# Totals of the softmax denominators by three bf16 products of exact pieces instead of one fp32 product

## The chip, the cores and the metric

The kernel runs on one core of a Trainium2 chip. A core has five engines with instruction queues of their own: PE (TensorE, matrix products into PSUM), DVE (VectorE), ACT (ScalarE), POOL (GpSimd) and SP (SyncE, which here issues most DMAs). They wait for each other by semaphores. The metric is the device time of one execution in microseconds; the time of the kernel before is the median of three runs.

## The reference, cut to what matters

Eight batches of eight heads, 576 positions and 64 values a head; a block-causal attention with blocks of 64, whose output is the input of a gated MLP without a nonlinearity.

```python
def _attn_ref(q, k, v):
    scores = scale * np.matmul(q, k.transpose(0, 1, 3, 2))
    scores = np.where(mask, scores, -1000000000.0)
    scores = scores - np.max(scores, axis=-1, keepdims=True)
    attn = np.exp(scores)
    attn = attn / (np.sum(attn, axis=-1, keepdims=True) + 1e-09)
    return np.matmul(attn, v)

def _moe_ref(x, w1, w2, w3, w_out):
    a = x @ w1
    b = x @ w2
    h = a * b @ w3
    return h @ w_out
```

The sum over the last axis of `attn` is the denominator that this case is about.

## The kernel before, in words

All products that need more than the rounded fp32 type of TensorE (`fp32r`) are made from a high and a low piece: `xh`, `xl` for the MLP's input, `w1h`, `w1l` for a weight, `ph`, `pl` for the exponentials. The work runs over 32 pairs of heads (`pair(n)`, four to a batch), and in a pair over its two heads `j`. Pairs 0 to 3 are "early": beside their attention the weights are unpacked and `w3 @ w_out` is multiplied out. From pair 4 on the attention of pair n runs beside the MLP of the batch before.

The order of PE is written out by hand: `PLAN` is a string of steps for each head, and each step takes one piece of work from a generator. `S` makes a tile of scores and its exponentials, `U` and `V` a piece of exponentials times values, `M` a piece of the row maxima of the next pair, `F` a piece of the MLP (24 a pair; half a batch of the MLP, 288 columns, is 48 of them: 32 of the two products `ab` at L426, then 16 of the product `o` at L442). `R`, `N` and `T` end a head: `R` is `sums`, `N` is `take`, `T` is `total`, `norm` and `finish_x`. The plan of the second head ends with `F R T M F F`. The other engines' instructions stand in the order in which the program issues them, as the scheduler places them.

The denominators from pair 4 on: POOL adds up the exponentials of a head in `rsum` (L286). `R` (L333, DVE) sums `rsum`, turned in blocks of 32 by 32, into 18 columns of `part`, one half for each head. `T` multiplies `part`, 128x36 in fp32, by `groups4` (four by four identities of 32x32 beside the identity, in the tile `ident`), which adds up the four groups of partitions into `tot` in PSUM (L337, PE). DVE copies `tot` into `rr` (L339), takes the reciprocal (L355), spreads it by a transpose (L357) and multiplies it into `x32` (L358); `finish_x` splits the result into `xh` and `xl` (L367 on ACT, L368 on POOL).

Around these stand: the row maxima `m` of the next pair (L196, L198 on DVE) and their transpose `mt` (L200, PE); `take` (L351 on ACT, L352 on DVE); the MLP's gate `g` (L433, DVE) with its high and low piece `gh` (L434, ACT) and `gl` (L435, POOL); the low piece of the queries and keys (L235, POOL, 64x1152) and of the values (L248, POOL).

Of the kernel before, what the change touches and what calls it, by code (L numbers as in the profile page):

```python
# [10 lines left out]
BF16 = mybir.dt.bfloat16  # L11
# [4 lines left out]
ALU = mybir.AluOpType  # L16
# [3 lines left out]
P = 128  # L20
B, H, S, D = 8, 8, 576, 64
# [46 lines left out]
def block_causal_attention__then__gated_mlp_kernel(ctx, tc, qkv, consts, ident_in, w1, w2, w3t, wout, out_t):  # L68
    nc = tc.nc
# [4 lines left out]
    work = ctx.enter_context(tc.tile_pool(name="work", bufs=1))  # L74
# [8 lines left out]
    ident, groups4 = both[:, 0:P], both[:, P:]  # L83
# [33 lines left out]
    tl = {}  # L117
# [9 lines left out]
    def open_late():  # L127
        pool = ctx.enter_context(tc.tile_pool(name="late", bufs=1, reuse_waits="tile"))
        tl["late"] = pool
        tl["ph"] = pool.tile([P, PW], F32R, name="ph")  # L130
        tl["sum"] = pool.tile([P, S], F32, name="rsum")
        tl["pl"] = pool.tile([P, PW], F32R, name="pl")

        tl["vs"] = [pool.tile([P, 5, P], F32R, name=f"vs{j}") for j in range(2)]
        tl["gh"] = pool.tile([P, NF, HALF], F32R, name="gh")
        tl["gl"] = pool.tile([P, NF, HALF], F32R, name="gl")
# [197 lines left out]

    def total(n, part, rr):
        tot = ps_q.tile([P, 512], F32, tag="psq", name=f"tot{n}")
        nc.tensor.matmul(tot[:, 0 : S // 16], groups4, part, start=True, stop=True)  # L337
        for j in range(2):
            nc.vector.tensor_scalar_add(rr[own[j]], tot[own[j], j * S // 32 : (j + 1) * S // 32], 1e-9)  # L339

# [127 lines left out]
    def pair(n):  # L468
# [9 lines left out]
        for j in range(2):  # L478
# [5 lines left out]
            for step in (EARLY_PLAN[n] if early else PLAN)[j].split():  # L484
# [3 lines left out]
                with tc.high_priority(offset=0) if early else nullcontext():  # L488
                    if step == "S":
                        fill(tiles, 1)  # L490
                    elif step == "F":
                        if delay:
                            delay -= 1
                        else:
                            fill(mlp, 1)
                    elif step == "M":
                        fill(masks, 1)
                    elif step == "A":
                        fill(next_qk, 1)
                    elif step == "B":  # L500
                        fill(own_qk, 1)
                    elif step in "UV":
                        fill(pvs, 1)
                    elif step == "R":
                        sums(n, j, part)
                    elif step == "N" and early:
                        take_early(n, j, xps, x32, rr)
                    elif step == "N":
                        take(n, j, xps, x32)
                    elif step == "T":  # L510
                        if not early:
                            total(n, part, rr)
                        norm(n, x32, rr)
                        finish_x(n, x32)
                    elif step == "Q" and not last:
                        if n + 1 != NPAIR:
                            prep_v(n + 1, j)
                        if j == 1 and n + 2 < NN:
                            load(n + 2)
# [4 lines left out]
    fill(prod, 100)  # L524
    wstack.close()
    open_late()
    for j in range(2):
        prep_v(NPAIR, j)
# [60 lines left out]
```

## Time and profile before

| what | value |
|---|---|
| median of three runs | 980.52 us (980.49 to 980.68) |
| the profiled execution | 982.55 us |
| its span, first to last instruction | 980.6 us |
| mean granted TensorE clock | 0.993 |
| from the `tot` of pair 4 (171.7 us) to that of pair 31 (896.7 us) | 27 pairs, 26.9 us each |
| `tot` (L337), two passes a pair | 56 products, 234 ns median each, beside 56 weight loads of 188 ns |
| L333, the reduction into `part` | 56, 43.0 us in all |
| L339, `tot` into `rr` | 56, 175 ns median |

A row of the profile's timeline gives the start in us from the beginning of the span, the duration, the engine, the line of the kernel, the operation, the tiles written and read, the shapes, how many instructions were merged into the row, and in brackets how long the engine stood idle before it and what released it. Products on PE overlap: a product of 288 columns is shown with 0.29 us and the next starts 0.13 us behind it. PEld rows are the loads of the weights, beside PE.

### The profile page before, as it was taken

The numbers are of one execution on the slowest core, as the hardware profiler recorded it, in microseconds if no ns is written. First come the engines' busy times: TensorE is split into PE (matmuls) and PEld (weight loads), VectorE is DVE, ScalarE is ACT, GpSimd is POOL, SyncE is SP. The second block draws the span as 40 slices with busy tenths as digits, with TensorE's granted clock in tenths as the row PEclk, the third lists the DMA queues.
The fourth block names the chain that finished last, engine by engine and source line by source line (L and its number), as shares of the span: only waits on it lengthen the run. The fifth ranks groups of instructions, "written<-read, shape, count | busy, mean of one in ns | idle before, by whom it ended". The sixth has DMA issues, their size and how long they took to land.

```text
span 980.6 us, 18312 instructions
## 1 busy us (share of the span) xinstructions
PE 941.6 (96%) x6594; PEld 879.1 (90%) x6624; DVE 692.4 (71%) x1230; ACT 557.3 (57%) x1451; POOL 629.6 (64%) x605
## 2 busy tenths in 40 slices
PE   3788989999999999999999999999999999999998
PEld 1444449999999999999999999999999999999998
DVE  6776857777777778878777777788787877774100
ACT  6776635656556665566565556655656555553221
POOL 6786737767676767677676767676776767673211
PEclk9999989999999999999999999999999999999999
DMA  8967502222222221222222221211222222100000
GB/s 294 304 198 221 163 19 62 63 75 63 87 63 75 63 87 41 66 69 65 73 66 83 64 80 57 88 54 53 69 72 66 69 81 63 50 13 25 7 19 25
DMA packets 31303, 79.81 MB, mean 81 GB/s; under 512 B 5356, under 2 KB 13676, under 8 KB 31212
## 3 DMA queue, kind: packets, MB, share of 16 engines
q1 hardware_dynamic: 29788, 76.26, 25.4%
q10 hardware_dynamic: 1424, 2.38, 1.0%
q8 instruction: 52, 0.85, 0.4%
q14 instruction: 39, 0.32, 0.1%
HBM read 50.76 MB, written 9.44 MB: 61 GB/s over the span
## 4 chain that ended last, share of the span: by engine, by line
PE 88%; ACT 3%; DVE 3%; POOL 3%; issue 2%; DMA 1%; ACTq 0%; SPq 0%; POOLq 0%; DVEq 0%
PE ab L426 42%; PE o L442 21%; PE s L265 9%; PE x L320 9%; PE mx L192 3%; PE w L407 2%; POOL wbits L152 1%; ACT wbits L151 1%; DMA wraw<-in_w 1%; ACT wy L150 1%; POOL w2l L162 1%; PE x L304 1%; DVE m L196 1%; ACT pe L273 1%; DVE qk L166 0%
## 5 line engine op out<-in xcount | busy, mean ns | idle before, releaser
L286 POOL TENSOR_TENSOR rsum<-rsum,p 128x448 f32<-128x448 f32 x224 | 186.1, 831 | 87.1 <-ACT p L280 76.8
L435 POOL TENSOR_TENSOR gl<-g,gh 128x288 fp32r<-128x288 f32 x128 | 114.5, 895 | 121.5 <-ACT gh L434 121.5
L283 DVE TENSOR_TENSOR pl<-p,ph 128x448 fp32r<-128x448 f32 x168 | 149.1, 901 | 60.1 <-ACT ph L281 59.2
L265 PE MATMUL s<-qk 128*128 128x288 f32 (+4 forms) x768 | 157.3, 314 | 16.3 <-ACT pe L273 10.8
L235 POOL TENSOR_TENSOR qk<-raw,qk 64x1152 fp32r<-64x1152 f32 x58 | 154.9, 2670 | 9.1 <-issue 6.1
L426 PE MATMUL ab<-xh,w2h 128*128 128x288 f32 x512 | 153.8, 300 | 0.0
L442 PE MATMUL o<-gh,wh 128*128 128x288 f32 x512 | 153.6, 300 | 0.0
L426 PE MATMUL ab<-xh,w1h 128*128 128x288 f32 x512 | 151.1, 295 | 0.0
L426 PE MATMUL ab<-xl,w2h 128*128 128x288 f32 x512 | 151.0, 295 | 0.0
L426 PE MATMUL ab<-xl,w1h 128*128 128x288 f32 x512 | 151.0, 295 | 0.0
L426 PE MATMUL ab<-xh,w1l 128*128 128x288 f32 x512 | 151.0, 295 | 0.0
L442 PE MATMUL o<-gh,wl 128*128 128x288 f32 x512 | 150.9, 295 | 0.0
L426 PE MATMUL ab<-xh,w2l 128*128 128x288 f32 x512 | 150.9, 295 | 0.0
L442 PE MATMUL o<-gl,wh 128*128 128x288 f32 x512 | 150.8, 295 | 0.0
L265 PEld LDWEIGHTS s<-qk 128*128 128x128 f32 (+1 forms) x768 | 116.9, 183 | 28.5 <-ACT pe L273 16.1
L434 ACT CAST gh<-g 128x288 fp32r<-128x288 f32 x128 | 55.4, 433 | 142.8 <-DVE g L433 142.7
L281 ACT ACTIVATE ph<-s 128x288 fp32r<-128x288 f32 x336 | 131.4, 393 | 0.0
L196 DVE TENSOR_REDUCE m<-mx 128x1 f32<-128x64 f32 (+3 forms) x320 | 128.3, 446 | 3.0 <-PE mx L192 0.8
L280 ACT ACTIVATE p<-s 128x448 f32<-128x448 f32 x224 | 85.5, 382 | 51.5 <-PE s L265 50.7
L283 DVE TENSOR_TENSOR pl<-rsum,ph 128x288 fp32r<-128x288 f32 x112 | 75.7, 677 | 49.2 <-ACT ph L281 45.4
L320 PE MATMUL x<-ph,vs 128*128 128x128 f32 x336 | 110.4, 329 | 0.0
L433 DVE TENSOR_TENSOR g<-ab,a 128x288 f32<-128x288 f32 x128 | 56.5, 441 | 69.5 <-PE ab L426 68.6
(76 smaller groups left out, 2182.4 us busy)
## 6 DMA issues: line engine op xcount, KB each, us to landing
raw<-in_qkv SPq DMA_DIRECT2D x31, 896.0 KB
qk<-qk SPq DMA_DIRECT2D x108, 144.0 KB
out_t<-o SPq DMA_DIRECT2D x64, 144.0 KB
wraw<-in_w3t SPq DMA_DIRECT2D x16, 512.0 KB
wraw<-in_w SPq DMA_DIRECT2D x16, 512.0 KB
wraw<-in_wout SPq DMA_DIRECT2D x8, 512.0 KB
qk<-qk ACTq DMA_DIRECT2D x16, 144.0 KB
qk<-ms SPq DMA_DIRECT2D x54, 2.2 KB
```

Source lines behind the costliest of these rows:

```text
L196: nc.vector.reduce_max(m[:, col : col + 1], sc, axis=AX.X)
L235: (nc.gpsimd if "late" in tl or n * j else nc.vector).tensor_tensor(out=qk[j][o, 2:4], in0=rqk[o], in1=qk[j][o, 0:2], op=ALU.subtract)
L265: nc.tensor.matmul(t[ks, at : at + q1 - q0], qk[j][:, k, kr], qk[j][:, q, q0:q1], start=(s == 0), stop=(s == 1))
L280: nc.scalar.activation(p32, t[ks, at : at + w], AF.Exp, scale=SCALE)
L281: nc.scalar.activation(ph[ks, o : o + w], t[ks, at : at + w], AF.Exp, scale=SCALE)
L283: nc.vector.tensor_tensor(out=low, in0=p32, in1=ph[ks, o : o + w], op=ALU.subtract)
L286: nc.gpsimd.tensor_tensor(out=r, in0=r, in1=p32, op=ALU.add)
L320: nc.tensor.matmul(xps[:, to : to + w], v[:, c, :], pr[:, a : a + w], start=(u < 2 and s == 0), stop=(u in (0, len(PV) - 1) and s == len(p ...
L426: nc.tensor.matmul(t[:, 0:HALF], l[:, c, fs], r, start=(c == 0 and s == 0), stop=(c == NC - 1 and s == 2))
L433: nc.vector.tensor_tensor(out=g32, in0=acc[1][:, 0:HALF], in1=a32, op=ALU.mult)
L435: nc.gpsimd.tensor_tensor(out=gl[:, f, :], in0=g32, in1=gh[:, f, :], op=ALU.subtract)
L442: nc.tensor.matmul(t[:, 0:HALF], l[:, f, es], r[:, f, :], start=(f == 0 and s == 0), stop=(f == NF - 1 and s == 2))
```

## The change

`part` is taken apart into three pieces of 16 bits. The first is `part` rounded to bf16; what is left is formed in place in `part`; its rounding is the second piece, and what is left then is the third. Each piece is exact, and their sum is `part`. `tot` is the sum of three bf16 products of `groups` (the same 0 and 1, copied once to bf16 by POOL when the late tiles are opened) with the pieces, accumulated in PSUM.

```diff
         tl["pl"] = pool.tile([P, PW], F32R, name="pl")
 
+        tl["groups"] = pool.tile([P, P], BF16, name="groups")
+        nc.gpsimd.tensor_copy(tl["groups"], groups4)
         tl["vs"] = [pool.tile([P, 5, P], F32R, name=f"vs{j}") for j in range(2)]
...
     def total(n, part, rr):
         tot = ps_q.tile([P, 512], F32, tag="psq", name=f"tot{n}")
-        nc.tensor.matmul(tot[:, 0 : S // 16], groups4, part, start=True, stop=True)
+        parts = work.tile([P, 3, S // 16], BF16, tag="parts", name=f"parts{n}")
+        part = part.rearrange("p j b -> p (j b)")
+        for i in range(2):
+            nc.vector.tensor_copy(parts[:, i, :], part)
+            rest = part if i == 0 else parts[:, 2, :]
+            nc.vector.tensor_tensor(out=rest, in0=part, in1=parts[:, i, :], op=ALU.subtract)
+        for i in range(3):
+            nc.tensor.matmul(tot[:, 0 : S // 16], tl["groups"], parts[:, i, :], start=(i == 0), stop=(i == 2))
         for j in range(2):
             nc.vector.tensor_scalar_add(rr[own[j]], tot[own[j], j * S // 32 : (j + 1) * S // 32], 1e-9)
```

The new instructions have the lines L342 (cast), L344 (subtraction) and L346 (product) of the changed kernel; its lines up to L133 are those of before, L135 to L337 there are two higher than before, and from L348 on nine higher.

DVE in pair 18 (the order is alike in pairs 4 to 30 with an even number), from the last maxima to the sum of `x`; before, with the semaphores' engines that a row waits for:

```order
L196 TENSOR_REDUCE m_6438<-mx_5_6604 128x1
L333 TENSOR_REDUCE part_6324<-rsum 128x18 [waits Pool_49]
L433 TENSOR_TENSOR g_6623<-ab,a_6621 128x288 [waits DVE_49,PE_49]
L198 TENSOR_TENSOR m_6438<-m_6438 128x1 [waits DVE_49]
L352 TENSOR_TENSOR x_18_6322<-x_1_6492,xlow_1_6643 64x576 [waits Activation_49]
```

and of the change:

```order
L198 TENSOR_REDUCE m_6538<-mx_5_6704 128x1
L335 TENSOR_REDUCE part_6424<-rsum 128x18 [waits Pool_49]
L442 TENSOR_TENSOR g_6723<-ab,a_6721 128x288 [waits DVE_49,PE_49]
L342 CAST parts_6759<-part_6424 128x36 [waits DVE_49]
L200 TENSOR_TENSOR m_6538<-m_6538 128x1
L344 TENSOR_TENSOR part_6424<-part_6424,parts_6759 128x36 [waits DVE_49]
L342 CAST parts_6759<-part_6424 128x36 [waits DVE_49]
L344 TENSOR_TENSOR parts_6759<-part_6424,parts_6759 128x36 [waits DVE_49]
L361 TENSOR_TENSOR x_18_6422<-x_1_6592,xlow_1_6743 64x576 [waits Activation_49]
```

The first cast stands ahead of the last step of the maxima (L198 before, L200 now), the other three behind it, and each of the four waits for DVE's own result ahead of it.

DVE in pair 17 (alike in the pairs 5 to 29 with an odd number), of the change:

```order
L335 TENSOR_REDUCE part_6048<-rsum 128x18 [waits Pool_49]
L200 TENSOR_TENSOR m_6166<-m_6166 128x1 [waits DVE_49]
L342 CAST parts_6378<-part_6048 128x36 [waits DVE_49]
L344 TENSOR_TENSOR part_6048<-part_6048,parts_6378 128x36 [waits DVE_49]
L342 CAST parts_6378<-part_6048 128x36 [waits DVE_49]
L344 TENSOR_TENSOR parts_6378<-part_6048,parts_6378 128x36 [waits DVE_49]
L361 TENSOR_TENSOR x_17_6046<-x_1_6220,xlow_1_6363 64x576 [waits Activation_49]
```

Here all four stand behind the last step of the maxima; before, nothing stood between it and L352. In pair 31, which has no maxima to make, the four stand right behind the reduction.

PE in pair 18, before:

```order
L426 MATMUL ab<-xl_1_4805,w2h 128x288
L337 MATMUL tot_6658<-part_6324,ident 128x36
L200 MATMUL mt_6675<-ident,m_6438 9x128 [waits DVE_49]
L426 MATMUL ab<-xh_1_5178,w2h 128x288
```

and of the change:

```order
L435 MATMUL ab<-xl_1_4877,w2h 128x288
L346 LDWEIGHTS groups
L346 MATMUL tot_6758<-parts_6759,groups 128x36 [waits DVE_49]
L346 LDWEIGHTS groups
L346 MATMUL tot_6758<-parts_6759,groups 128x36 [waits DVE_49]
L346 LDWEIGHTS groups
L346 MATMUL tot_6758<-parts_6759,groups 128x36 [waits DVE_49]
L202 MATMUL mt_6782<-ident,m_6538 9x128
L435 MATMUL ab<-xh_1_5257,w2h 128x288
```

One fp32 product, which the chip runs as two passes with their own weight loads, has become three bf16 products, and each of the three waits for its piece. Nothing else changed its place on any engine; on POOL the copy of `groups` stands ahead of the first L248 of the late pairs.

## The prediction, made before the changed kernel ran

> **What bounds the kernel now.** I read the busy times first, then the busy times by stage, then the timeline around the totals (`tot`), engine by engine.
>
> ```profile
> PE 941.6 (96%) x6594; PEld 879.1 (90%) x6624; DVE 692.4 (71%) x1230; ACT 557.3 (57%) x1451; POOL 629.6 (64%) x605
> ```
> ```profile
> 198.60:870.70 672.10, 672.06 (x5053) 664.24 (x5077) 524.11 (x950) 399.62 (x1098) 468.21 (x450) 1.00 0.23 67
> ```
> The second row runs from the `tot` of pair 5 to that of pair 30: 25 pairs, 26.88 us each, and PE (first number after the comma) is busy in 672.06 of 672.10 us, at full clock (1.00). PE stands still nowhere between two totals, so nothing there can absorb a stall of PE: each 0.1 us that PE waits in a pair comes out at the end, and each 0.1 us less of PE work too. DVE, at 71%, is not the bound; what DVE work costs depends only on whether PE waits for it.
>
> (Its columns: busy us and instructions of PE, weight loads, DVE, ACT and POOL, then clock, DMA share and GB/s.)
>
> The place is step T of the second head. Half a batch of the MLP is 48 F steps, two pairs long, so pairs alternate: the totals of even pairs fall into the `ab` products (L426), those of odd pairs into the `o` products (L442). PE in an even pair (18), then an odd one (17); the columns are start, duration, engine, line, operation:
>
> ```profile
> 548.07 0.29 PE L426 MATMUL ab<-xl,w2h 128*128 128x288 f32 x1
> 548.20 0.31 PE L337 MATMUL tot<-part,ident 128*128 128x36 f32 x2
> 548.34 0.28 PE L200 MATMUL mt<-ident,m 128*9 128x128 f32 x1
> 548.37 0.38 PE L426 MATMUL ab<-xh,w2h 128*128 128x288 f32 x1
> 548.59 0.30 PE L426 MATMUL ab<-xh,w2l 128*128 128x288 f32 x1
> ```
> ```profile
> 521.35 0.30 PE L337 MATMUL tot<-part,ident 128*128 128x36 f32 x2
> 521.49 0.28 PE L200 MATMUL mt<-ident,m 128*9 128x128 f32 x1
> ```
> Products start 0.13 us apart and `tot` falls into that beat: PE doesn't wait for it. DVE and POOL at the same places, odd pair first:
>
> ```profile
> 519.24 0.77 DVE L333 TRANSPOSE_TENSOR_REDUCE part<-rsum 128x18 f32<-128x576 f32 x1
> 519.94 0.82 DVE L198 TENSOR_TENSOR m<-m 128x1 f32<-128x1 f32 x1
> ```
> ```profile
> 518.07 2.67 POOL L235 TENSOR_TENSOR qk<-raw,qk 64x1152 fp32r<-64x1152 f32 x1
> 521.93 0.88 POOL L248 TENSOR_TENSOR vs<-raw,vs 128x320 fp32r<-128x320 f32 x1 [1.19 <-ACT vs L166]
> ```
> ```profile
> 546.10 0.77 DVE L333 TRANSPOSE_TENSOR_REDUCE part<-rsum 128x18 f32<-128x576 f32 x1
> 546.79 0.42 DVE L433 TENSOR_TENSOR g<-ab,a 128x288 f32<-128x288 f32 x1
> 547.13 0.47 DVE L198 TENSOR_TENSOR m<-m 128x1 f32<-128x1 f32 x1
> 548.66 0.76 DVE L352 TENSOR_TENSOR x<-x,xlow 64x576 f32<-64x576 f32 x1 [1.05 <-ACT xlow L351]
> ```
> ```profile
> 544.92 2.67 POOL L235 TENSOR_TENSOR qk<-raw,qk 64x1152 fp32r<-64x1152 f32 x1
> 547.82 0.80 POOL L435 TENSOR_TENSOR gl<-g,gh 128x288 fp32r<-128x288 f32 x1 [0.23 <-ACT gh L434]
> ```
> Count from the end of L333 (520.01 and 546.87) as zero. PE reaches `tot` at 1.34 (odd) and 1.33 (even), and `mt` at 1.48 and 1.47. **That 1.33 us is the room for the split.** It is partly taken: L198 works on one element, yet lasts 0.82 and 0.47 us, and in both pairs ends at 0.73 to 0.75, just when POOL's L235 ends (520.74, 547.59).
>
> ```profile
> L198 DVE TENSOR_TENSOR m<-m x32: 143/488/1220, 13.7 to 869.6; 128x1 f32<-128x1 f32 x32
> L283 DVE TENSOR_TENSOR ph<-p,ph x56: 228/502/512, 157.2 to 893.3; 64x64 fp32r<-64x64 f32 x56
> L161 DVE CAST w2h<-wy x8: 405/976/989, 88.9 to 123.7; 128x512 fp32r<-128x512 f32 x8
> ```
> Minimum, median and maximum in ns: the same L198 takes 143 free and 488 here. So a DVE operation with both inputs in SBUF stands still while POOL's subtraction runs, and ends some 0.02 us behind it. The Trainium skill ("SBUF — State Buffer", Who interferes with whom) gives the rule: VectorE and GpSimd share a port pair, held exclusively by whoever starts first for its whole instruction; the trace agrees by these L198 rows.
>
> **The change, part by part.** Four DVE instructions of 128x36 come between L333 and the last product: cast, subtract, cast, subtract, each waiting for the one ahead. A one-element operation is 143 ns, the 64-element subtraction 228 at best, so 36 elements come to 143 + 35 x 85/63 = 0.19 us. The cast of 512 elements (L161) takes 405 at best, so (405 - 143)/511 = 0.51 ns an element, less than half of the subtraction's 1.35, and 36 elements come to 143 + 35 x 0.51 = 0.16 us. Its median is 976 while POOL works on the weights: such a cast is held up too, and I take it that the new one is. Between dependent operations lie 0.03 to 0.04 us, and from a DVE end to the PE start it releases some 0.05:
>
> ```profile
> 522.54 0.27 DVE L355 RECIPROCAL rr<-rr 128x18 f32<-128x18 f32 x1
> 522.84 0.78 DVE L357 STREAM_TRANSPOSE rb<-rr 128x576 f32<-128x576 f32 x1
> ...
> 13.68 0.16 DVE L198 TENSOR_TENSOR m<-m 128x1 f32<-128x1 f32 x1
> ...
> 13.89 0.09 PEld L200 LDWEIGHTS mt<-ident,m 128*9 128x9 f32 x1 [1.32 <-DVE m L198]
> ```
> *Odd pairs (13, 5 to 29).* L198 stands ahead of the split and ends at 0.75; the cast, independent of it, may start 0.07 earlier, as L198 did behind L333. Cast 0.67 to 0.83, subtract 0.87 to 1.06, cast 1.09 to 1.25, subtract 1.28 to 1.47; POOL's next, L248, comes only at 1.92. Third product at 1.52, `mt` 0.04 behind it at 1.56, where it stood at 1.48: +0.08. Bounds: all four at 143 give `mt` at 1.43 (-0.05); all four at 0.27 (L355, the nearest dependent small operation, slower per element) give +0.45. I take +0.08, since L198 and L283 are the nearest in kind: 13 x 0.08 = 1.0 us.
>
> *Even pairs (14, 4 to 30).* The first cast stands ahead of L198. It is ready at 0.27, waits for L235 until 0.72 and ends at 0.76. L198 runs to 0.83, the first subtraction from 0.80 to 0.99. Now POOL's L435 is due at 0.95 (547.82). It takes the ports when that subtraction lets go, about 0.99, and keeps them 0.80, until 1.79. The second cast, ready at 1.03, waits and ends at 1.83; the second subtraction 1.86 to 2.05; third product 2.10, `mt` 2.14 instead of 1.47: +0.67. L435 comes 0.23 behind L235 in the first and the last of the 14:
>
> ```profile
> 171.34 0.80 POOL L435 TENSOR_TENSOR gl<-g,gh 128x288 fp32r<-128x288 f32 x1 [0.23 <-ACT gh L434]
> ...
> 870.27 0.81 POOL L435 TENSOR_TENSOR gl<-g,gh 128x288 fp32r<-128x288 f32 x1 [0.23 <-ACT gh L434]
> ```
> 14 x 0.67 = 9.4 us. Bounds: if L435 lets the split go first, the second subtraction ends at 1.41 and `mt` stands at 1.50, +0.03; with operations of 0.27 and L435 ahead, +0.75.
>
> Whether the cast is held decides the size. If not, the first ends at 0.46, the second runs 0.91 to 1.10 beside L435, and only the second subtraction waits, until L435 ends at 1.75: 1.81, product 1.86, `mt` 1.90, +0.43. The Trainium skill ("VectorE: DVE Perf Modes", What auto-detection actually checks) lets a one-source operation from SBUF to SBUF with even sizes use both ports, whatever the types; by it the first sum holds, and L161's 405 and 976 ns agree for another type.
>
> *PE's own work.* `tot` was two passes, 0.14 us up to `mt`. Two bf16 products of 64 and 256 columns take 0.07 between them:
>
> ```profile
> 543.42 0.32 PE L192 MATMUL mx<-kb,qd 128*128 128x64 bf16 x2
> 543.49 0.45 PE L320 MATMUL x<-ph,vs 128*128 128x448 f32 x1
> ```
> Three would take 0.11, a gain of 0.03 a pair, from nothing to all 0.14 at the bounds. Where PE waits for the last part, the first two products lie in the wait and the gain is void; only pair 31 keeps it:
>
> ```profile
> 893.61 0.78 DVE L333 TRANSPOSE_TENSOR_REDUCE part<-rsum 128x18 f32<-128x576 f32 x1
> 896.70 0.30 PE L337 MATMUL tot<-part,ident 128*128 128x36 f32 x2
> ```
> There PE comes 2.31 us behind the reduction: 0.0 to -0.1.
>
> *What is queued behind.* On PE `mt`, then L426 or L442, all later by the stall; ScalarE's copy of `mt` and the mask's DMA too, but their reader on PE is later by as much. On DVE L352 waits behind the split: it was due at 1.79 (548.66) and comes at 2.06, 0.27 later, while PE is 0.67 later, so it costs nothing further. `groups` is one POOL cast before the first L248, in an idle stretch of 6.10 us, so nothing; uncovered it is under the 0.85 us of one L248.
>
> ```profile
> 150.01 1.70 POOL L248 TENSOR_TENSOR vs<-raw,vs 128x320 fp32r<-128x320 f32 x2 [6.10 <-ACT vs L166]
> ```
> **Sum:** 9.4 + 1.0 - 0.1 = +10.3 us. Against the profiled execution, 982.55 us with a span of 980.6, that is 992.85; it lies 2.0 above the median of the timed runs, 980.52, to which I add the same: 990.8 us.
>
> **Rivals.**
> 1. *Casts are not held by POOL.* Even pairs +0.43; in odd pairs casts of 0.19 make it +0.14: 6.0 + 1.8 = +7.8, 988.3. For it: no DVE cast to bf16 stands in this trace. Against: L161.
> 2. *L435 doesn't get between.* If POOL, asking at 0.95, is kept off until all four are through, then 14 x 0.03 + 13 x 0.08 = +1.4, 981.9: no change that a measurement could tell. Against: in L198 the one who came first kept the ports.
> 3. *Faster: the split beats PE.* It is done before 1.30, so PE never waits and keeps its gain. It would need four operations and their gaps within 0.58 us of L235's end (0.72), 0.12 each, below L198's 143 ns, and POOL kept off as in 2; then three products within 0.05 give -0.09 a pair, -2.5, 978.0.
> 4. *Dearer operations*, 0.27 each: 14 x 0.75 + 13 x 0.45 = +16.4, 996.9. For it: L355. Against: its operation is another.
>
> **How the numbers follow.** Forecast 0.54, rival 1 0.27, rival 2 0.10, rival 3 0.04, rival 4 0.05. The range leaves out 2, 3 and 4, 0.19 in all: from 985 (rival 1 with every operation at 143: 14 x 0.38 - 13 x 0.05 = +4.7) to 994 (forecast with odd pairs halfway to their upper bound). A measurement of this kernel tells a change above about 0.2%, 2 us. Faster 0.04, same 0.10, slower 0.86.
>
> **What would show it.** PE idle ahead of the last product of `tot`, released by DVE, about 0.6 us in even pairs and 0.1 in odd; in even pairs a second cast of 0.8 us that ends with L435 (forecast), or a second subtraction of 0.7 (rival 1); L435 at 0.95 to 1.0; no new wait elsewhere. The forecast is wrong if the split in even pairs ends before 1.5 us, or if PE's beat beside it has gaps that give time back.

## The result, and the profile after

| | before | changed |
|---|---|---|
| median | 980.52 us | 992.21 us |
| lowest to highest | 977.25 to 981.5 | 990.88 to 992.47 |
| runs | 5 | 5 |
| span of the profiled execution | 980.6 us | 990.2 us |
| first total (pair 4) to last total (pair 31) | 171.67 to 896.70: 725.0 us | 171.65 to 906.30: 734.7 us |
| last total to the end of the span | 83.9 us | 83.9 us |

The changed kernel is slower: ratio 1.0121 with a 95% interval of 1.0102 to 1.0140. Nothing changed ahead of the first total or behind the last; all of the loss lies in the 27 pairs between.

The same stretch of the busy times by stage, in the changed kernel, from the total of pair 5 to that of pair 30:

```profile
199.10:879.80 680.70, 675.86 (x5102) 663.14 (x5100) 548.97 (x1050) 398.35 (x1098) 468.35 (x450) 1.00 0.23 66
```

PE was busy in all but 0.04 us of it before and now stands idle for 4.8 us. The list of who waited for whom, from 195 us on, has one entry for PE, and it is new:

```profile
PE tot L346 <- DVE parts L342: 4.4, 14, 0.4
```

Fourteen waits: the even pairs from 6 to 30, which are thirteen, and one odd pair, 23. (Pair 4, whose total is at 171.7 us, lies ahead of this stretch and waits as well: fifteen in all.) The 0.2 to 0.4 us of each are not the whole stall, since the products ahead of it are drawn with their pipelined ends and cover its beginning. The stall is read from the starts: summed over the 27 pairs, the time from the first product of `tot` to `mt` is 14.3 us instead of 3.7, so 10.6 us more. PE in pair 18, and then in pair 17 (start, duration, engine, line, operation):

```profile
552.70 0.29 PE L435 MATMUL ab<-xl,w2h 128*128 128x288 f32 x1
552.84 0.19 PE L346 MATMUL tot<-parts,groups 128*128 128x36 bf16 x1
553.36 0.41 PE L346 MATMUL tot<-parts,groups 128*128 128x36 bf16 x2 [0.33 <-DVE parts L342]
553.62 0.27 PE L202 MATMUL mt<-ident,m 128*9 128x128 f32 x1
553.64 0.38 PE L435 MATMUL ab<-xh,w2h 128*128 128x288 f32 x1
```

```profile
525.91 0.39 PE L346 MATMUL tot<-parts,groups 128*128 128x36 bf16 x3
526.15 0.27 PE L202 MATMUL mt<-ident,m 128*9 128x128 f32 x1
```

From the first product of `tot` to `mt` it was 0.14 us in both pairs; now it is 0.78 in the even one and 0.24 in the odd one. The first of the three products runs in the old place, and the other two stand behind DVE. DVE and POOL in pair 18:

```profile
550.74 0.77 DVE L335 TRANSPOSE_TENSOR_REDUCE part<-rsum 128x18 f32<-128x576 f32 x1
551.43 0.42 DVE L442 TENSOR_TENSOR g<-ab,a 128x288 f32<-128x288 f32 x1
551.78 0.51 DVE L342 CAST parts<-part 128x36 bf16<-128x36 f32 x1
552.20 0.15 DVE L200 TENSOR_TENSOR m<-m 128x1 f32<-128x1 f32 x1
552.32 0.20 DVE L344 TENSOR_TENSOR part<-part,parts 128x36 f32<-128x36 f32 x1
552.55 0.76 DVE L342 CAST parts<-part 128x36 bf16<-128x36 f32 x1
553.34 0.20 DVE L344 TENSOR_TENSOR parts<-part,parts 128x36 bf16<-128x36 f32 x1
553.57 0.76 DVE L361 TENSOR_TENSOR x<-x,xlow 64x576 f32<-64x576 f32 x1
```

```profile
549.57 2.67 POOL L237 TENSOR_TENSOR qk<-raw,qk 64x1152 fp32r<-64x1152 f32 x1
552.46 0.80 POOL L444 TENSOR_TENSOR gl<-g,gh 128x288 fp32r<-128x288 f32 x1 [0.22 <-ACT gh L443]
```

Two casts of the same size are side by side here with what held them. The first lasts 0.51 us and ends at 552.29, behind POOL's L237 (552.24). The second lasts 0.76 us, from 552.55 to 553.31, and POOL's `gl` (L444) runs from 552.46 to 553.26. In the odd pair, where POOL is idle by then, a cast takes 0.17 to 0.18 us:

```profile
525.22 0.17 DVE L342 CAST parts<-part 128x36 bf16<-128x36 f32 x1
525.43 0.20 DVE L344 TENSOR_TENSOR part<-part,parts 128x36 f32<-128x36 f32 x1
525.66 0.18 DVE L342 CAST parts<-part 128x36 bf16<-128x36 f32 x1
525.88 0.20 DVE L344 TENSOR_TENSOR parts<-part,parts 128x36 bf16<-128x36 f32 x1
```

Pair 23 is the one odd pair that is not like this. POOL, DVE and PE there:

```profile
686.27 2.68 POOL L237 TENSOR_TENSOR qk<-raw,qk 64x1152 fp32r<-64x1152 f32 x1
```

```profile
687.05 0.77 DVE L335 TRANSPOSE_TENSOR_REDUCE part<-rsum 128x18 f32<-128x576 f32 x1
687.75 1.23 DVE L200 TENSOR_TENSOR m<-m 128x1 f32<-128x1 f32 x1
688.89 0.17 DVE L342 CAST parts<-part 128x36 bf16<-128x36 f32 x1
```

```profile
689.83 0.27 PE L202 MATMUL mt<-ident,m 128*9 128x128 f32 x1
```

L237 ends at 688.95, 1.13 us behind the reduction (687.82) instead of 0.73. It holds L200 that long, the split behind L200 starts as much later, and `mt` stands at 2.01 instead of 1.48.

### The profile page after: what moved, and what is told of

Its sections match the earlier page's. It is cut to its first block, busy times and chain, and to the rows that moved or that the text cites. A ratio compares the mean times of both kernels' runs of the same rounds, so it can differ in the third digit from the quotient of the medians.

```text
span 990.2 us, 18511 instructions
## 1 busy us (share of the span) xinstructions
PE 945.7 (96%) x6652; PEld 878.2 (89%) x6652; DVE 722.8 (73%) x1342; ACT 555.9 (56%) x1451; POOL 629.1 (64%) x606
## 4 chain that ended last, share of the span: by engine, by line
PE 79%; DVE 10%; ACT 4%; DMA 3%; POOL 2%; issue 2%; ACTq 0%; SPq 0%; POOLq 0%; DVEq 0%
PE ab L435 37%; PE o L451 20%; PE s L267 9%; PE x L322 6%; PE mx L194 3%; DVE m L198 2%; PE w L416 2%; DVE parts L342 2%; DMA qk<-ms 1%; ACT wbits L153 1%; DVE part L335 1%; DVE pl L285 1%; DMA wraw<-in_w 1%; POOL w2l L164 1%; POOL wbits L154 1%
## 5 line engine op out<-in xcount | busy, mean ns | idle before, releaser
L444 POOL TENSOR_TENSOR gl<-g,gh 128x288 fp32r<-128x288 f32 x128 | 114.1, 892 | 125.3 <-ACT gh L443 125.3
L267 PE MATMUL s<-qk 128*128 128x288 f32 (+4 forms) x768 | 157.7, 315 | 16.3 <-ACT pe L275 10.8
L237 POOL TENSOR_TENSOR qk<-raw,qk 64x1152 fp32r<-64x1152 f32 x58 | 154.8, 2670 | 9.1 <-issue 6.1
L198 DVE TENSOR_REDUCE m<-mx 128x1 f32<-128x64 f32 (+3 forms) x320 | 128.5, 447 | 3.0 <-PE mx L194 1.0
```

What stands on the lines that cost most here:

```text
L198: nc.vector.reduce_max(m[:, col : col + 1], sc, axis=AX.X)
L237: (nc.gpsimd if "late" in tl or n * j else nc.vector).tensor_tensor(out=qk[j][o, 2:4], in0=rqk[o], in1=qk[j][o, 0:2], op=ALU.subtract)
L267: nc.tensor.matmul(t[ks, at : at + q1 - q0], qk[j][:, k, kr], qk[j][:, q, q0:q1], start=(s == 0), stop=(s == 1))
L444: nc.gpsimd.tensor_tensor(out=gl[:, f, :], in0=g32, in1=gh[:, f, :], op=ALU.subtract)
```

## The experiments

Theory L: the loss is PE's wait for the split, and in the even pairs it is long because POOL's `gl` holds the second cast, which means that the cast stands still until `gl` has ended. Rivals: the three products cost PE their own time (P), DVE's added work delays the rest of the attention (D), four dependent operations are long whoever else runs (C), a wait that is taken away comes out elsewhere (E). Times are compared with runs of the kernel before on the same chip: medians of 982.03 us for e1, e2, e3 and e4 and 981.80 for e3b, e5 and e6. Each edit is shown against the changed kernel, cut to what matters.

### e1: the products alone

The split is left out, the products read a tile that is written once.

```diff
-        parts = work.tile([P, 3, S // 16], BF16, tag="parts", name=f"parts{n}")
-        part = part.rearrange("p j b -> p (j b)")
-        for i in range(2):
-            nc.vector.tensor_copy(parts[:, i, :], part)
...
+        parts = tl["parts"]
```

> The split is left out: the three bf16 products read a tile of ones that is written once, so no product waits for VectorE and the denominators are wrong. Theory L (the loss is PE's wait for the split, which POOL's lock on the shared ports makes long): no wait at the totals; each total is some 0.045 us shorter than before, as in pair 31 of the changed kernel, so the span is 980.6 - 28 x 0.045 = 979.3 us. Rival P (the three products with their weight loads cost PE the time themselves): span stays near 990.

Measured: 981.23 us, ratio 0.9995 (0.998 to 1.0009); span 978.0, from the first total to the last 724.2 us. No wait at any total. Rival P is out: the products as such cost nothing. PE in pair 31:

```profile
894.43 0.24 PE L343 MATMUL tot<-parts,groups 128*128 128x36 bf16 x3
894.52 0.38 PE L448 MATMUL o<-gh,wh 128*128 128x288 f32 x1
```

Three bf16 products take 0.09 us to the next one, where the two fp32 passes took 0.14. That is the gain of 0.05 a pair. By the starts it adds up to 1.3 us over the 27 pairs, too small to be told in the time.

### e2: the split beside the total

All four DVE operations run, on a tile `left` of their own, and nothing reads their result; the total is the fp32 product of before.

```diff
+        left = work.tile([P, S // 16], F32, tag="left", name=f"left{n}")
...
-        for i in range(3):
-            nc.tensor.matmul(tot[:, 0 : S // 16], tl["groups"], parts[:, i, :], start=(i == 0), stop=(i == 2))
+        nc.tensor.matmul(tot[:, 0 : S // 16], groups4, part, start=True, stop=True)
```

> The four VectorE operations run as in the change, on a tile of their own, and their result is left unused; the total is the one fp32 product of before and waits for the reduction alone. Theory L: VectorE's extra work is off PE's path, the second cast of the even pairs is still held by POOL (0.75 us), and the span is that of before, 980.6 (980 to 981.5). Rival D (the extra VectorE work or its blocking of POOL delays the rest of the attention): span 985 to 990.

Measured: 984.36 us, ratio 1.0023 (1.0010 to 1.0037); span 982.7. Neither as expected: most of the loss is gone, but not all. There is no wait at the totals. The list of waits names another place:

```profile
PEld ab L435 <- DVE g L442: 2.9, 12, 0.3
```

The kernel before has a single such wait, of 0.2 us, in the same list. Pair 18 shows how it comes about, DVE first and then the weight load for PE:

```profile
548.88 0.20 DVE L345 TENSOR_TENSOR parts<-left,parts 128x36 bf16<-128x36 f32 x1
549.09 0.76 DVE L361 TENSOR_TENSOR x<-x,xlow 64x576 f32<-64x576 f32 x1
...
554.14 0.99 DVE L285 TENSOR_TENSOR pl<-rsum,ph 128x288 fp32r<-128x288 f32 x1 [1.45 <-ACT ph L283]
555.05 0.45 DVE L442 TENSOR_TENSOR g<-ab,a 128x288 f32<-128x288 f32 x1
```

```profile
555.55 0.19 PEld L435 LDWEIGHTS ab<-xh,w2h 128*128 128x128 f32 x1 [0.24 <-DVE g L442]
```

The held split ends 2.0 us behind the reduction, so the sum of `x` (L361) starts 0.24 us later than before, counted from the reduction, and with it the reciprocal, the normalized `x`, ScalarE's two copies `xh`, the exponentials behind them on ScalarE's queue, the subtraction that reads them, and the gate `g` queued behind that on DVE. `g` frees the accumulator that the next `ab` products wait for. Rival D is real, at 0.24 us in an even pair, but it is a price of its own and not the changed kernel's: there PE itself comes 0.63 us late, and the wait doesn't appear in its list (a single 0.2, as before).

### e3 and e3b: without the `gl` that holds the cast

In both POOL's low piece of the gate is left out for one f tile in batches 0 to 6 and stands as written once at the start.

```diff
-                nc.gpsimd.tensor_tensor(out=gl[:, f, :], in0=g32, in1=gh[:, f, :], op=ALU.subtract)
+                if f != 3 or b == B - 1:
+                    nc.gpsimd.tensor_tensor(out=gl[:, f, :], in0=g32, in1=gh[:, f, :], op=ALU.subtract)
```

In e3 the tile was 4 instead of 3.

> The changed kernel without POOL's low piece of the gate for the fifth of eight f tiles in batches 0 to 6, the one that falls between the split's second and third operation in the even pairs; that part of the product with the low piece is left out. Theory L: the second cast of the even pairs takes 0.18 instead of 0.75 us, the split ends near 1.48 us behind the reduction and PE waits some 0.1 us as in the odd pairs; each even pair loses 0.11 instead of 0.63, span 990.2 - 14 x 0.52 = 982.9. Rival C (four dependent operations are long by themselves, whoever else runs): span stays near 990.

Measured: 990.21 us, ratio 1.0086 (1.0059 to 1.0113), and 734.8 us from the first total to the last. This is a miss, of the aim and not of the theory: in its trace `gl` still starts 0.95 us behind the reduction in thirteen of the fourteen even pairs. The fifth tile's gate is finished only behind the total; the one that runs there belongs to the fourth, which DVE gets to late. As a whole e3 says nothing on L or C, except that a POOL operation taken away elsewhere leaves the loss as it is.

Its one other pair, 14, says something all the same. There `gl` happens to start 0.29 us later, just behind the second cast. DVE, then POOL:

```profile
441.75 0.18 DVE L344 CAST parts<-part 128x36 bf16<-128x36 f32 x1
441.96 0.84 DVE L346 TENSOR_TENSOR parts<-part,parts 128x36 bf16<-128x36 f32 x1
```

```profile
441.95 0.79 POOL L447 TENSOR_TENSOR gl<-g,gh 128x288 fp32r<-128x288 f32 x1 [0.52 <-ACT a L442]
```

The cast takes 0.18 us, and it is the last subtraction, 0.20 us elsewhere, that lasts 0.84 and ends 0.06 us behind `gl`. So neither operation is long by itself; the one that meets `gl` is.

> As e3, but it is the fourth f tile whose low piece is left out: e3's trace showed the one that holds the ports untouched, since the fifth tile's falls behind the total. Theory L: the second cast of the even pairs takes 0.18 us, the split ends near 1.5, PE waits 0.1: from the first total to the last 734.7 - 14 x 0.52 = 727.4 us. Rival C (four dependent operations are long by themselves): stays at 734.7.

Measured: 983.93 us, ratio 1.0019 (1.0001 to 1.0037), span 980.8, 726.9 us from the first total to the last. DVE in pair 18:

```profile
546.72 0.20 DVE L346 TENSOR_TENSOR part<-part,parts 128x36 f32<-128x36 f32 x1
546.95 0.18 DVE L344 CAST parts<-part 128x36 bf16<-128x36 f32 x1
547.17 0.20 DVE L346 TENSOR_TENSOR parts<-part,parts 128x36 bf16<-128x36 f32 x1
547.71 0.76 DVE L363 TENSOR_TENSOR x<-x,xlow 64x576 f32<-64x576 f32 x1 [0.34 <-ACT xlow L362]
```

The same cast takes 0.18 us, the split is through 1.45 us behind the reduction, and DVE stands free again before `x`. The stretch is 7.7 us shorter than in the changed kernel, 14 x 0.55. Rival C would have left it. Together with the miss of e3, where a `gl` of another tile was left out and the loss stayed, this is the experiment that shows the cause: 14 operations of POOL, which neither read nor write anything of the totals, were four fifths of the loss.

### e4: the total two F steps later

Step T is moved behind the next two F steps, but for the last pair of each batch.

```diff
+            if n % NPAIR != NPAIR - 1:
+                plan = plan.replace("R T M F F", "R M F F T")
```

> The changed kernel with step T two F steps later (R M F F T instead of R T M F F), but for the last pair of each batch, whose output the MLP needs soonest. Theory L: PE reaches the total some 1.6 us later than before, behind the split's end at 2.1, and waits nowhere in 21 pairs; 6 odd pairs keep 0.11 each; each of the 21 gains 0.045 by its products: span 980.6 + 0.7 - 1.0 = 980.3. Rival E (what the wait hides comes out elsewhere, since the chain behind the total is late as well): span 984 to 990.

Measured: 982.34 us, ratio 0.9997 (0.9983 to 1.0011); span 981.4. With the same split, the second cast held as before (0.69 us in pair 18) and the same products, the times no longer tell the kernel from the one before: it is the moment at which PE asks that was changed.

The trace has a remainder. First to last total, 725.0 us, is no fair measure here, since the first total was moved later and the last was not. From the end of pair 4's reduction to that of pair 31's it is 725.8 us, where the kernel before has 724.0 and the changed one 733.7: 7.9 of 9.7 us are gone. Of the 1.8 that are left, pair 23, whose total was not moved, has some 0.5, the five other odd pairs that keep their place have 0.1 each, and one wait is new:

```profile
PE s L267 <- DMA qk<-ms: 0.6, 1, 0.6
```

It stands ahead of the scores of pair 30, behind the transfer of their row maxima (`ms`), and makes that pair 0.8 us longer. So rival E, which expected a span of 984 to 990, is out as the fate of the loss; whether this one wait comes from the later totals is not shown. The 0.05 us that each of the 21 moved totals should gain do not show in the 1.8 either; where they went is open.

### e5: two pieces

The third piece and its product are left out, so that the denominators keep 16 bits or so.

```diff
+        nc.vector.tensor_copy(parts[:, 0, :], part)
+        nc.vector.tensor_tensor(out=parts[:, 1, :], in0=part, in1=parts[:, 0, :], op=ALU.subtract)
...
+        for i in range(2):
+            nc.tensor.matmul(tot[:, 0 : S // 16], tl["groups"], parts[:, i, :], start=(i == 0), stop=(i == 1))
```

> The third piece and its product are left out (the denominators keep some 16 bits): one cast, one subtraction, two products. Theory L: the subtraction ends 1.0 us behind the reduction in the even pairs, before POOL's low piece of the gate takes the ports, and 1.07 in the odd ones, both before PE comes at 1.34; no wait, DVE is free again before the sum of x at 1.8, and each pair is shorter than before by 0.05 plus one product of 0.03: from the first total to the last 725.0 - 27 x 0.07 = 723.1 us (before 725.0, changed kernel 734.7), ratio to before 0.998. Rival C (bf16 pieces are slow as such, whatever POOL does): a wait stays at the totals, half of the 9.7 us or so.

Measured: 981.40 us, ratio 0.9996 (0.9983 to 1.0010), 725.1 us from the first total to the last. PE in pair 18:

```profile
546.74 0.22 PE L344 MATMUL tot<-parts,groups 128*128 128x36 bf16 x2
546.80 0.27 PE L202 MATMUL mt<-ident,m 128*9 128x128 f32 x1
```

The list has no wait, and it is 0.06 us from `tot` to `mt` instead of 0.14, as expected; only in pair 23, behind its late L237, does the second product come some 0.1 us late. The 2 us that this should give do not show in the time. They are there at the totals: summed over the 27 pairs, from the first product of `tot` to the product behind the last it is 1.8 us instead of 3.7. But the rest of the stretch took 723.2 us instead of 721.3. In this execution PE's products came more slowly: between neighbouring products of `ab` or of `o` the mean step from start to start is 133.56 ns in the stretch, before 133.04, 0.4% more, and the work behind the last total, which no experiment touches, took 84.3 us (895.35 to 979.62) where it took 83.9 before. Over the stretch 0.4% is some 3 us, more than the gain. What sets this pace is not shown; the interval of the ratio reaches 1.7 us below no change, so whether the time gains stays open.

### e6: the `gl` made twice

```diff
+                for _ in range(2 if f == 3 and b < B - 1 else 1):
```

> The changed kernel with that low piece (fourth f tile, batches 0 to 6) made twice in a row by POOL. Theory L: one more hold of the ports of 0.8 us; if the second comes ahead of the waiting cast, the cast ends at 2.6 and each even pair loses 0.8 more (first to last total 745.9 us); if the cast gets in between, the last subtraction waits instead, 0.6 more (743). Rival C: stays at 734.7.

Measured: 991.66 us, ratio 1.0101 (1.0076 to 1.0126), 734.7 us from the first total to the last: that of the changed kernel, and neither of the two figures that L was thought to give. DVE and POOL in pair 18:

```profile
553.08 0.76 DVE L342 CAST parts<-part 128x36 bf16<-128x36 f32 x1
553.88 0.20 DVE L344 TENSOR_TENSOR parts<-part,parts 128x36 bf16<-128x36 f32 x1
```

```profile
553.00 1.74 POOL L445 TENSOR_TENSOR gl<-g,gh 128x288 fp32r<-128x288 f32 x2 [0.23 <-ACT gh L443]
```

The waiting cast goes in between the two, as one of the two cases had it, but the second `gl` doesn't hold the subtraction: it starts 0.08 us behind the end of the first, and the subtraction 0.04 us behind the end of the cast. The two start within 0.01 us of each other, the subtraction first, and it runs its usual 0.20 us; the second `gl` takes some 0.85 instead of 0.80. A second POOL operation beside the split costs nothing here; what counts is which of the two has started when the other comes. As it is the changed kernel with work added that costs it nothing, it also repeats the change's time: ratio 1.0101, where the change itself had 1.0121.

## Why the prediction was right

The forecast was 990.8 us, and 992.21 was measured. Its steps, one by one:

- **Where PE comes to the total, and that it absorbs nothing.** Right: the waits at the totals are the only new ones of PE, and the part behind the last total is as long as before.
- **Even pairs.** Forecast +0.67 us, from the cast's start at 1.03 behind the reduction, its end at 1.83 and the last subtraction's end at 2.05. The trace has 552.55, 553.31 and 553.54 against a reduction that ends at 551.51: 1.04, 1.80 and 2.03, and `mt` is later by 0.64. e3b shows that `gl` is the cause. Two details came out otherwise. The forecast let `gl` wait for the first subtraction and run from 0.99 to 1.79; its row has 0.95 to 1.75, as before the change, though the subtraction ends at 1.00, and that is most of the 0.03 by which the cast ended sooner. And PE's idle time was to stand ahead of the last product; most of it stands ahead of the second, which needs the held cast.
- **Odd pairs.** Forecast +0.08, measured in pair 17 0.24 - 0.14 = 0.10 from `tot` to `mt`, 0.11 from the reduction. The operations were 0.01 to 0.02 dearer than 0.16 and 0.19.
- **The cast is held like a two-input operation.** The rival that denied it priced the even pairs at +0.43 and the sum at 988.3. The rows of pair 18 decide: the second cast ends 0.05 us behind POOL's `gl`, the first as much behind L237, and free of POOL it takes 0.18. The runs show the hold and what ends it; that it is the shared ports through which POOL holds DVE is the prediction's reading, and no run here tests it.
- **PE's own gain, void but for pair 31.** Right: there the next product stands 0.09 us behind the first of `tot` (906.30 to 906.39) instead of 0.14 (896.70 to 896.84), -0.05.
- **DVE's lateness costs nothing further.** Right in the changed kernel, by the reason given, that PE is later still; e2 shows its price of 0.24 us in an even pair when PE is on time.
- **One odd pair with a long wait.** Not forecast: in pair 23 L237 ran 0.4 us later than in the others, and the pair lost 0.53 us. The forecast took all odd pairs to be like pair 17, though the kernel before had the same late L237 (its L235) in that pair, where it cost nothing. In other executions it is another pair (19 in that of e3b, 5 in those of e3 and e6).

With the sizes of pairs 17 and 18, 14 x 0.64 + 12 x 0.11 + 0.53 - 0.05 is 10.8 us; the stalls of the 27 pairs summed from the starts are 10.6, and the forecast's sum was 10.3. That the sum comes so near is in part luck: the even pairs were priced 0.03 too high, fourteen times, and the odd ones 0.03 too low, twelve times, with 0.45 missing in pair 23.

The two profiled spans differ by 9.6 us and the medians by 11.7; the interval of the ratio, 10.0 to 13.7 us, holds the sum and just misses the difference of the spans. The stalls account for more than that difference because the rest of the stretch took 720.3 us instead of 721.3. PE's pace is enough for this 1.0: the mean step between products of `ab` or of `o` is 132.71 ns in the changed kernel's execution and 133.04 in that of before, 0.25%.

The split of the pairs was right: all fourteen even pairs stand behind `gl`, no odd one does, and leaving out the fourteen `gl` took 7.7 us of the loss away. That the 0.11 in the odd pairs is the length of the chain behind L237's end rests on the rows of pair 17 and on pair 23, where L237 ends 0.41 us later and `mt` comes 0.42 us later than in pair 17; no run undid L237.

## What to carry to other kernels

Before moving a small product's work from the bound engine to an idle one, count the dependent steps behind the last input and compare with how long the bound engine takes to arrive: here 1.33 us of room for a chain of some 0.85 us, of which POOL's two operations left too little. An engine's share of busy time says nothing about this; DVE had 29% idle. If the result is needed later than it is asked for, ask later: two F steps (e4) undid the loss as far as the times can tell, and four fifths of it by the trace.

## What the runs showed that was not expected

- DVE's lateness of 0.24 us beside the total reaches PE some 6.5 us later through ScalarE's queue and the gate (e2: twelve waits, 2.9 us), although nothing reads the delayed result. PE's 672.06 of 672.10 us busy hid how near the edge that place was.
- When POOL's operation ends, a DVE cast that it held goes ahead of POOL's next operation, which starts 0.08 us behind the last, in all fourteen even pairs (e6).
- PE's work behind the last total took between 83.6 and 84.3 us in the executions of nine kernels that don't differ there. In e5 the slower pace hid a gain of 2 us that its own totals show.
